# Turning the last block of outputs in two halves and storing it from two queues

## The chip, the cores and the metric

The kernel runs on one core of one Trainium2 chip. The metric is the device time of one execution in microseconds (us). The kernel before takes 943.23 us as the median of three runs (943.13 to 943.5). In this kernel TensorE does the matrix products, VectorE and ScalarE work on elements, and SyncE issues transfers. The program's tiles lie in two memories, SBUF and PSUM, and TensorE writes its products to tiles in PSUM. A transfer between SBUF and `out` is called a DMA, and the profile shows it as packets on 16 DMA engines (139,777 packets in the kernel before).

## The reference

An attention over pooled keys and values, followed by a feed-forward block with a snake activation. Cut to what matters:

```python
q, k, v: (8, 8, 576, 64)            # batch, heads, sequence, head dimension
k_p, v_p = mean of 8 neighbouring rows of k, v
x = softmax(q @ k_p.T / 8) @ v_p    # -> (4608, 512)
h = x @ w_in                        # w_in: (512, 2048)
g = h + sin(alpha * h)**2 / (alpha + 1e-9)
return g @ w_out                    # w_out: (2048, 512) -> out (4608, 512) float32
```

Only the end of the last product, `g @ w_out`, is touched by the change.

## The kernel before

The last product is computed for 8 groups of 576 output rows (`u`). Each group is made of 2 x 2 blocks by a scheme of seven products (`p`) with seven sub-products each, whose sums and differences are combined on VectorE. A finished block `t` lies in SBUF as 128 partitions (output columns, permuted) by `h` (2), `i` (2), `c` (T = 144 rows). VectorE turns it in 32 x 32 blocks into `o`, and four stores, one for each 32 partitions, write it to `out`:

```python
def out(u, i, j, t):
    o = self.op.tile([P, 2 * T // 32, 2, 32], F32, name="o", bufs=3)
    nc.vector.transpose(out=o[:].rearrange("p n h c -> p h n c"),
                        in_=t[:].rearrange("p h i c -> p h (i c)").rearrange("p h (n c) -> p h n c", c=32))
    r = u * self.S + i * 2 * T
    for a in range(4):
        c = j * 2 * P + a * 64
        nc.sync.dma_start(out=self.out[r:r + 2 * T, c:c + 64].rearrange("(n k) c -> k n c", k=32),
                          in_=o[32 * a:32 * a + 32].rearrange("k n h c -> k n (h c)"))
```

One store moves 72 KB in 288 pieces of 256 bytes (the trace has 1152 packets of 256 bytes for the last four). The block that ends last is that of the seventh product (`p == 3`), `i = 0, j = 1`:

```python
def early(st):                       # while the last products still run
    t = C[st["u"]]["c"]
    with_z(t, st["yz"])
    add(t[:, :, 1], t[:, :, 1], st["x1"][:])
# ... in combine(), for p == 3:
    t = c["c"]
    add(t[:, :, 0], t[:, :, 0], x[0][:])    # needs the last product; writes i = 0 of both h
    out(u, 0, 1, t)
# ... the order of the last products:
    fifth(); fourth()                # fourth() calls early(last)
    product(last, 2, last["x0"][:, 0, :], False)
    product(last, 3, last["x0"][:, 1, :], False)
    combine(last)
```

## Time and profile before

| | before |
|---|---|
| median time | 943.23 us |
| span, first to last instruction | 941.79 us |
| end of the last matmul | 936.07 us |
| from there to the end of the span ("the tail") | 5.72 us |
| TensorE busy | 98% of the span |

The tail is the number to follow, because the change touches nothing ahead of it. Its parts are read from the timeline, from the waits of the SyncE queue, and from the busy share of the DMA engines in stretches of 0.2 us. The lines of these views stand in the prediction.

### The profile page before, as it was taken

How to read it: one execution, taken by the hardware profiler on the slowest of the kernel's cores; microseconds unless marked ns; L12 is line 12 of the kernel's file. 1: busy time of each engine (PE TensorE's matmuls, PEld its weight loads, DVE VectorE, ACT ScalarE, POOL GpSimd, SP SyncE). 2: the span in 40 equal slices, each digit the busy share in tenths (PEclk: the TensorE clock that was granted, in tenths of full speed). 3: DMA queues.
4: the chain of work that ended last, by engine and by line, in shares of the span. 5: the costliest groups of instructions: out<-in, count | busy, mean ns of one | idle time of the engine just before them, and what ended most of it. 6: DMA issues, size and time to landing. Idle time of an engine off the chain costs nothing.

```text
span 941.8 us, 17546 instructions
## 1 busy us (share of the span) xinstructions
PE 920.8 (98%) x6859; PEld 819.5 (87%) x6859; DVE 694.5 (74%) x1043; ACT 445.6 (47%) x1042; POOL 197.9 (21%) x214
## 2 busy tenths in 40 slices
PE   5999999999999999999999999999999999999997
PEld 3687787887878878787888899999999999999997
DVE  5779584766748677484346889988989798889794
ACT  5477576585857758677696651212111111211111
POOL 1628354453634536250000000000000000000000
PEclk9999999999999999999999999999999999999999
DMA  9645457666576663745624545353435444343501
GB/s 230 178 142 173 122 190 167 201 160 201 154 195 194 167 191 101 186 148 146 224 90 143 187 141 150 103 164 89 148 105 135 118 127 127 117 135 93 160 13 38
DMA packets 139777, 137.82 MB, mean 146 GB/s; under 512 B 49024, under 2 KB 108176, under 8 KB 139696
## 3 DMA queue, kind: packets, MB, share of 16 engines
q1 hardware_dynamic: 138624, 135.53, 49.8%
q10 hardware_dynamic: 1072, 1.19, 0.5%
q8 instruction: 54, 0.88, 0.4%
q14 instruction: 27, 0.22, 0.1%
HBM read 74.46 MB, written 47.19 MB: 129 GB/s over the span
## 4 chain that ended last, share of the span: by engine, by line
PE 94%; DVE 2%; ACT 2%; DMA 1%; issue 0%; SPq 0%; ACTq 0%; DVEq 0%
PE bank L497 45%; PE bank L778 29%; PE ps_y L778 12%; PE ps_o L311 3%; PE ps_sc L210 2%; DMA q<-in_q_dram 1%; DVE as L373 1%; PE ps_qt L191 1%; PE ps_at L269 1%; ACT s L503 1%; PE bank L460 1%; DVE home L470 0%; PE ps_or L320 0%; PE bank L122 0%; DVE a L373 0%
## 5 line engine op out<-in xcount | busy, mean ns | idle before, releaser
L497 PE MATMUL bank<-home,a 128*128 128x256 f32 x1152 | 267.1, 383 | 0.8 <-ACT bank L535 0.8
L497 PEld LDWEIGHTS bank<-home,a 128*128 128x128 f32 x1152 | 214.8, 190 | 35.8 <-ACT bank L535 2.7
L497 PE MATMUL bank<-home,as 128*128 128x256 f32 x864 | 202.4, 383 | 1.2 <-DVE as L373 0.8
L497 PEld LDWEIGHTS bank<-home,as 128*128 128x128 f32 x864 | 161.2, 190 | 26.4 <-ACT bank L523 3.2
L107 POOL TENSOR_TENSOR kvin<-kvin 72x512 f32<-72x512 f32 x112 | 122.2, 1091 | 164.2 <-DMA kvin<-in_v_dram 108.8
L778 PE MATMUL bank<-s,wb 128*128 128x144 f32 x896 | 119.4, 286 | 0.4 <-ACT bank L891 0.4
L778 PEld LDWEIGHTS bank<-s,wb 128*128 128x128 f32 x896 | 113.7, 190 | 0.7 <-ACT bank L891 0.6
L510 ACT ACTIVATE s<-s,c 128x256 f32<-128x256 f32 (+1 forms) x216 | 110.0, 573 | 0.0
L503 ACT ACTIVATE s<-h,al 128x256 f32<-128x256 f32 x144 | 65.2, 501 | 79.6 <-DVE h L476 79.6
L476 DVE TENSOR_TENSOR h<-bank,p 128x512 f32<-128x512 f32 x72 | 49.2, 683 | 62.8 <-ACT s L510 28.2
L891 ACT COPY bank<-bank 128x144 f32<-128x144 f32 x56 | 14.7, 263 | 145.7 <-PE bank L778 144.3
L503 ACT ACTIVATE s<-bank,al 128x256 f32<-128x256 f32 x144 | 59.9, 467 | 33.5 <-PE bank L497 10.5
L564 DVE TENSOR_TENSOR h<-bank,s 128x512 f32<-128x512 f32 x36 | 24.6, 684 | 49.7 <-ACT s L510 49.0
L910 ACT COPY bank<-bank 128x144 f32<-128x144 f32 x56 | 14.7, 263 | 88.2 <-PE bank L778 88.2
L252 POOL TENSOR_TENSOR ex<-ex,sm 128x576 f32<-128x576 f32 (+1 forms) x38 | 42.7, 1148 | 60.0 <-DVE sm L251 29.1
L733 DVE TENSOR_TENSOR s<-r 128x576 f32<-128x576 f32 x64 | 48.1, 752 | 0.8
L564 DVE TENSOR_TENSOR h<-h,s 128x1024 f32<-128x1024 f32 x36 | 46.2, 1283 | 0.0
L733 DVE TENSOR_TENSOR s<-x 128x576 f32<-128x576 f32 x48 | 36.2, 753 | 7.6 <-PE ps_y L778 6.7
L868 ACT COPY bank<-ps_y 128x288 f32<-128x288 f32 x56 | 21.4, 383 | 38.7 <-PE ps_y L778 38.7
L147 DVE STREAM_TRANSPOSE tr<-q 128x1024 f32<-128x1024 f32 (+1 forms) x24 | 18.1, 808 | 26.8 <-DMA g_bridge<-h 21.3
L778 PE MATMUL bank<-s,a 128*128 128x144 f32 x256 | 36.6, 286 | 0.0
L778 PE MATMUL ps_y<-s,a 128*128 128x144 f32 x256 | 36.6, 286 | 0.0
(142 smaller groups left out, 1436.4 us busy)
## 6 DMA issues: line engine op xcount, KB each, us to landing
g_bridge<-h SPq DMA_DIRECT2D x72, 512.0 KB
r<-g_bridge SPq DMA_DIRECT2D x31, 1152.0 KB
out_dram<-o SPq DMA_DIRECT2D x128, 72.0 KB
q<-in_q_dram SPq DMA_DIRECT2D x8, 1024.0 KB
kvin<-in_k_dram SPq DMA_DIRECT2D x28, 288.0 KB
kvin<-in_v_dram SPq DMA_DIRECT2D x28, 288.0 KB
a<-in_moe_w_in_dram SPq DMA_DIRECT2D x16, 256.0 KB
q<-tr SPq DMA_DIRECT2D x48, 80.0 KB
```

Of the source, the lines that this page charges most:

```text
L107: (eng or nc.gpsimd).tensor_tensor(out=o, in0=t[:, :, 0:w], in1=t[:, :, w:2 * w], op=OP.add)
L210: nc.tensor.matmul(ps[e][r:r + q.shape[-1], hp, :], q[s], kb[s, hp, :], start=True, stop=True)
L252: eng.tensor_tensor(out=E(n, i, 0, H), in0=E(n, i, 0, H), in1=sm[:n].unsqueeze(2).to_broadcast([n, H, Sp]), op=OP.mult)
L311: nc.tensor.matmul(ps[64 * e:64 * e + 64, :], vp[:, h, :], x, start=True, stop=True)
L476: add = lambda o, x, y: nc.vector.tensor_tensor(out=o, in0=x, in1=y, op=OP.add)
L497: nc.tensor.matmul(ps[:, jj, :], self.A[p][:, kk, f * P:(f + 1) * P], x[:, kk, :], start=(start and jj == 0 and kk == 0), stop=(kk == 1), ...
L503: nc.scalar.activation(out=G.s[:, i, jj, j, :], in_=src[:, jj], func=AF.Sin, scale=self.al[:, f:f + 1])
L510: nc.scalar.activation(out=x, in_=x, func=AF.Square, scale=self.c[:, f:f + 1])
L564: add = lambda o, x, y: self.nc.vector.tensor_tensor(out=o, in0=x, in1=y, op=OP.add)
L733: tt = lambda o, x, y, op: nc.vector.tensor_tensor(out=o, in0=x, in1=y, op=op)
L778: nc.tensor.matmul(out, W[:, J // 2, J % 2, :], A[:, J, :], start=(start and J == 0), stop=(J == self.NJ - 1), skip_group_check=True)
L868: nc.scalar.copy(out=x0[:], in_=yz[:, 0:1, :].to_broadcast([P, 2, T]))
```

## The change

Its intent is to shorten the end: the last block is turned in two halves along `h`, and two of its four stores go to the queue of ScalarE, which is idle by then (its last copy ends at 932.45 us in the profile before).

```diff
             o = self.op.tile([P, 2 * T // 32, 2, 32], F32, name="o", bufs=3)
-            nc.vector.transpose(out=o[:].rearrange("p n h c -> p h n c"),
-                                in_=t[:].rearrange("p h i c -> p h (i c)").rearrange("p h (n c) -> p h n c", c=32))
+            end = (u, i, j) == (self.B - 1, 0, 1)
+            for h in (slice(0, 1), slice(1, 2)) if end else (slice(0, 2),):
+                nc.vector.transpose(out=o[:, :, h].rearrange("p n h c -> p h n c"),
+                                    in_=t[:, h].rearrange("p h i c -> p h (i c)").rearrange("p h (n c) -> p h n c", c=32))
             r = u * self.S + i * 2 * T
             for a in range(4):
                 c = j * 2 * P + a * 64
-                nc.sync.dma_start(out=self.out[r:r + 2 * T, c:c + 64].rearrange("(n k) c -> k n c", k=32),
+                (nc.scalar if end and a % 2 else nc.sync).dma_start(out=self.out[r:r + 2 * T, c:c + 64].rearrange("(n k) c -> k n c", k=32),
                                   in_=o[32 * a:32 * a + 32].rearrange("k n h c -> k n (h c)"))
```

## The prediction

Its rival (a) is that the issues of the two queues wait for each other; the pair of issues at 0.74 us is its test of that.

> **What bounds the kernel now.** I read the page first: the engine table, then the 40 slices, and after that only the end of the execution, because the diff touches nothing else (its condition is true for one block, the last of 32).
>
> ```profile
> PE 920.8 (98%) x6859; PEld 819.5 (87%) x6859; DVE 694.5 (74%) x1043; ACT 445.6 (47%) x1042; POOL 197.9 (21%) x214
> ```
>
> TensorE is busy for 98% of a span of 941.8 us. So the body is bound by matmuls, and a change that leaves them alone can only win in the few microseconds at the end in which TensorE has nothing left. The timeline of the last microseconds shows that stretch (start, duration, engine, line, operation):
>
> ```profile
> 934.93 1.14 PE L778 MATMUL bank<-s,wb 128*128 128x144 f32 x8
> 936.11 0.45 DVE L733 TENSOR_TENSOR cc<-cc,bank 128x288 f32<-128x288 f32 x1 [0.32 <-PE bank L778]
> 936.60 0.78 DVE L796 STREAM_TRANSPOSE o<-cc 128x576 f32<-128x576 f32 x1
> 937.40 1.85 SPq L801 DMA_DIRECT2D out_dram<-o  x4
> ```
>
> The last matmul ends at 936.07, then one add, one transpose and four stores follow strictly one after another, with gaps of 0.02 to 0.04 us. The stores' issue ends at 937.40 + 1.85 = 939.25. Cut finer, the four issues are one of 0.32 us (start 937.40) and three of about 0.46 to 0.47 (starts 937.76, 938.26, 938.78). What follows is in the waits of the SyncE queue after 930 us, and in the stretches of 0.2 us (columns: length, busy time of PE, weight load, DVE, ACT, POOL, clock, busy share of the 16 DMA engines, GB/s):
>
> ```profile
> SPq L1012 <- DMA out_dram<-o: 1.4, 1, 1.4
> ```
>
> ```profile
> 938.00:938.20 0.20, 0.00 (x0) 0.00 (x0) 0.00 (x0) 0.00 (x0) 0.00 (x0) 1.00 0.00 0
> 938.20:938.40 0.20, 0.00 (x0) 0.00 (x0) 0.00 (x0) 0.00 (x0) 0.00 (x0) 1.00 0.58 133
> 938.40:938.60 0.20, 0.00 (x0) 0.00 (x0) 0.00 (x0) 0.00 (x0) 0.00 (x0) 1.00 0.87 181
> 938.60:938.80 0.20, 0.00 (x0) 0.00 (x0) 0.00 (x0) 0.00 (x0) 0.00 (x0) 1.00 0.40 85
> ...
> 939.60:939.80 0.20, 0.00 (x0) 0.00 (x0) 0.00 (x0) 0.00 (x0) 0.00 (x0) 0.50 0.45 90
> 939.80:940.00 0.20, 0.00 (x0) 0.00 (x0) 0.00 (x0) 0.00 (x0) 0.00 (x0) 0.50 0.78 177
> 940.00:940.20 0.20, 0.00 (x0) 0.00 (x0) 0.00 (x0) 0.00 (x0) 0.00 (x0) 0.50 0.78 160
> 940.20:940.40 0.20, 0.00 (x0) 0.00 (x0) 0.00 (x0) 0.00 (x0) 0.00 (x0) 0.50 0.10 18
> ```
>
> The data starts about 938.23, so 0.83 after the first issue begins, and stops about 940.22. The share of the engines goes up and down with the issues: they are not kept full. Summed over all eleven stretches (0.58, 0.87, 0.40, 0.87, 0.70, 0.50, 0.89, 0.45, 0.78, 0.78, 0.10 = 6.92, times 0.2 us) the four stores cost 1.38 us of engine time, 0.346 each, but are handed over only every 0.49 us. So the tail is paced by the issue on one queue, and about 30% of the engines' time in it is idle. SyncE is released at about 940.66 and the span ends at 941.8; those last 1.1 us are the closing barrier, which the change doesn't touch. The chain view names an earlier store ahead of the last transpose; I don't believe it, since the timeline shows the add ending just there.
>
> [...] The trace agrees that issue time is real here (1.85 us of a 3.3 us stretch from first issue to release). [...] The trace before has one place to test it, the very start:
>
> ```profile
> 0.74 0.40 ACTq L333 DMA_DIRECT2D s<-in_moe_alpha_dram  x1
> 0.74 0.42 SPq L102 DMA_DIRECT2D home<-in_k_dram  x1
> ```
>
> Both begin together and neither is longer than it is alone (ScalarE's other issue, a load at 554.1, is 0.40 too)[...]; but the ScalarE load is of 8 KB in 16 rows, a weak test. [...] adds of 128x576 take about 0.755 us and of 128x288 about 0.455.
>
> **The change part by part.** *Transposes.* The compiled order has two transposes of 128x9x32 in place of one of 128x2x9x32. They are cut along h, but the last add writes both h, and each store reads both h of its 32 partitions. So neither half can start before the add ends, and no store can start before the second half ends: nothing is overlapped, and the cut only costs. Halving an add saves 0.755 - 0.455 = 0.30 us, so I take 0.778 - 0.30 = 0.478 for half a transpose (estimate). Two independent DVE instructions in a row overlap by about 0.08 in their windows (two 0.45 us adds show as 0.82). Pair: 2 x 0.478 - 0.08 = 0.876, against 0.778: **+0.10 us**, all on the path.
>
> *Stores.* Two of four issues move to ScalarE, idle since 932.45 (its last copy starts 932.19 and takes 0.26), so nothing stands ahead of them. Their waits in the compiled order are the transpose and two DMA semaphores last used by stores of at least ten microseconds before or by the block at 927, long landed. Let t be the first issue's start. Before: last issue ends t+1.85, data ends t+2.82. After: SyncE ends its two at t+0.32+0.04+0.46 = t+0.82, ScalarE at most t+0.9 (0.40 for its first). The second pair's data could then start at about t+0.82+0.5 = t+1.3. But two stores' data need 2 x 0.346 = 0.69 us from t+0.83, so until t+1.52 at the least: the pair is in time and the engines become the pace. All four: t+0.83+1.38 = t+2.21 with full engines, t+0.83+1.38/0.88 = t+2.40 at the 0.87 to 0.89 that the fullest stretches show. Middle t+2.30: **-0.52 us**. It isn't the 0.95 us by which the issues shorten, for the data now limits.
>
> *Sum:* +0.10 - 0.52 = **-0.42 us**, hence 943.23 - 0.42 = 942.8.
>
> **The rivals.** (a) [...] The two queues wait for each other and the four stores still come every 0.49 us. For it: [...]the first issue of 0.32 against 0.46 for those right behind it, as if something were being waited for. Against: the pair at 0.74. Time: +0.10, so 943.3. I give it 25%. (b) *Interleaving hurts.* The stores write neighbouring 256-byte pieces of the same output rows, and two queues would mix them; the engines' 1.38 us might grow. For it: nothing in the trace tests two queues of stores; against: the same 16 engines carried up to 406 GB/s near 559 us with larger pieces. Time: around 943.1. 15%. (c) *Engines drain better with both queues full,* under 0.346 per store: up to -0.7, so 942.5. 10%. (d) *The transposes hide,* or the compiler gains from the halves: excluded by the order of the add and the reads of the stores.
>
> **Range and chances.** Half the weight at 942.8, a quarter at 943.3, the rest around gives a mean near 942.9. Three runs before spread over 0.37 us (943.13 to 943.5), as much as the effect. Range 942.3 to 943.5. 2% is 18.9 us, and the whole tail after the last matmul is 941.8 - 936.07 = 5.7 us, so faster by over 2% is not possible by this path; slower would need a disturbance elsewhere, and all matmuls stand in the same order. Within 2%: 0.99.
>
> **What would show it.** In the profile after: two transposes of about 0.48 us with the first at the end of the add, the stores starting about 0.1 later relative to the last matmul (right), or one of them earlier (wrong). Two issues on SyncE and two on ScalarE starting together near 937.5, each 0.3 to 0.47 long; issues of 0.7 or more on either would show rival (a). Stretches of 0.2 us with a share near 0.9 without dips, ending 2.2 to 2.4 us after the first issue, would show the engines as the new pace; a summed share time well above 1.38 us would show (b). I'd be wrong if the data ends later than t+2.6, or if the span before 936 us moves.

## The result

The changed kernel takes 943.28 us (942.28 to 943.65, 4 runs), the kernel before in the same rounds 943.37 us (943.13 to 944.28, 4 runs). The ratio is 0.9996 with a 95% interval of 0.9978 to 1.0013. It is the mean time of one kernel's fast runs over that of the other's in the same rounds, so not quite the ratio of the two medians. By total time the two are the same.

The end of the profile is not the same. The timeline of the changed kernel, in which the two queues' issues are given by further looks at shorter windows (start, duration, engine, line, operation):

```profile
934.92 1.14 PE L778 MATMUL bank<-s,wb 128*128 128x144 f32 x8
936.10 0.46 DVE L733 TENSOR_TENSOR cc<-cc,bank 128x288 f32<-128x288 f32 x1 [0.32 <-PE bank L778]
936.59 0.84 DVE L798 STREAM_TRANSPOSE o<-cc 128x288 f32<-128x288 f32 x2
937.46 0.89 ACTq L803 DMA_DIRECT2D out_dram<-o  x2
```

```profile
937.46 0.32 SPq L803 DMA_DIRECT2D out_dram<-o  x1
937.46 0.38 ACTq L803 DMA_DIRECT2D out_dram<-o  x1
...
937.82 0.46 SPq L803 DMA_DIRECT2D out_dram<-o  x1
937.88 0.47 ACTq L803 DMA_DIRECT2D out_dram<-o  x1
```

The last matmul ends at 936.07, as before. The two halves take 0.84 us in place of 0.78, back to back. The issues on the two queues lie side by side, and all four are done at 938.35, where one queue had been busy until 939.25. The stretches of the DMA engines (columns as in the prediction; the last two are the busy share and GB/s) show what became of it:

```profile
938.20:938.40 0.20, 0.00 (x0) 0.00 (x0) 0.00 (x0) 0.00 (x0) 0.00 (x0) 1.00 0.33 74
938.40:938.60 0.20, 0.00 (x0) 0.00 (x0) 0.00 (x0) 0.00 (x0) 0.00 (x0) 1.00 0.91 196
938.60:938.80 0.20, 0.00 (x0) 0.00 (x0) 0.00 (x0) 0.00 (x0) 0.00 (x0) 1.00 0.91 192
938.80:939.00 0.20, 0.00 (x0) 0.00 (x0) 0.00 (x0) 0.00 (x0) 0.00 (x0) 1.00 0.81 132
939.00:939.20 0.20, 0.00 (x0) 0.00 (x0) 0.00 (x0) 0.00 (x0) 0.00 (x0) 1.00 0.81 132
939.20:939.40 0.20, 0.00 (x0) 0.00 (x0) 0.00 (x0) 0.00 (x0) 0.00 (x0) 1.00 1.17 254
939.40:939.60 0.20, 0.00 (x0) 0.00 (x0) 0.00 (x0) 0.00 (x0) 0.00 (x0) 1.00 1.17 257
939.60:939.80 0.20, 0.00 (x0) 0.00 (x0) 0.00 (x0) 0.00 (x0) 0.00 (x0) 1.00 0.97 208
939.80:940.00 0.20, 0.00 (x0) 0.00 (x0) 0.00 (x0) 0.00 (x0) 0.00 (x0) 1.00 0.15 31
```

The dips to 0.40 to 0.50 between stores are gone: from 938.4 to 939.8 the share never falls under 0.8, and the data ends in the stretch that begins at 939.8 instead of the one at 940.2. By the records, the tail is 5.17 us (941.23 - 936.07) against 5.72: **0.55 us shorter**, somewhat more than the 0.42 us that the sum of the prediction gave. The next question is whether this is real, which of the two parts makes it, and why the total time doesn't show it.

### The profile page after: what moved, and what is told of

It is laid out like the page before. It is cut to its first block, busy times and chain, and to the rows that moved or that the text cites. A ratio compares the mean times of both kernels' runs of the same rounds, so it can differ in the third digit from the quotient of the medians.

```text
span 941.2 us, 17548 instructions
## 1 busy us (share of the span) xinstructions
PE 921.0 (98%) x6859; PEld 819.7 (87%) x6859; DVE 692.9 (74%) x1044; ACT 445.9 (47%) x1042; POOL 199.1 (21%) x214
## 3 DMA queue, kind: packets, MB, share of 16 engines
q10 hardware_dynamic: 1680, 1.34, 0.6%
## 4 chain that ended last, share of the span: by engine, by line
PE 95%; DVE 2%; ACT 1%; DMA 1%; issue 0%; SPq 0%; DVEq 0%; ACTq 0%
PE bank L497 45%; PE bank L778 29%; PE ps_y L778 12%; PE ps_o L311 3%; PE ps_sc L210 2%; DMA q<-in_q_dram 1%; PE ps_qt L191 1%; PE ps_at L269 1%; PE bank L460 1%; DVE as L373 0%; DVE home L470 0%; PE ps_or L320 0%; PE bank L122 0%; ACT s L503 0%; PE bank L210 0%
## 5 line engine op out<-in xcount | busy, mean ns | idle before, releaser
L778 PE MATMUL ps_y<-r,wb 128*128 128x144 f32 x256 | 36.6, 286 | 0.0
L778 PE MATMUL bank<-r,wb 128*128 128x144 f32 x256 | 36.6, 286 | 0.0
```

Of the source, the lines that this page charges most:

```text
L778: nc.tensor.matmul(out, W[:, J // 2, J % 2, :], A[:, J, :], start=(start and J == 0), stop=(J == self.NJ - 1), skip_group_check=True)
```

## The experiments

The theory: the halves cost a few hundredths and bring nothing; the second queue brings the whole gain, because one queue hands over a store only about every 0.5 us while the engines need 0.35 us for it; with two queues the data itself is the pace. The rivals: the halves let something start sooner; the issues of the two queues wait for each other; neighbouring pieces written by two queues disturb each other.

Four kernels ran on one chip, four more on the same chip, and the two that are cut by rows on another. This table gathers the profiles of all but the last three, which have their own sections; times from the records in us, "issue" is the start of the first of the last block's stores after the end of the last matmul, "data" the time from the first to the last packet of these stores, "engine time" the sum of their packets' durations divided by 16 (up to 24 packets are under way at once on the 16 engines in the changed kernel, so it is not quite the time in which the engines were busy).

| kernel | last matmul ends | span | tail | issue | data | engine time |
|---|---|---|---|---|---|---|
| before | 936.07 | 941.79 | 5.72 | 1.33 | 2.08 | 1.39 |
| before, again | 936.14 | 941.86 | 5.72 | 1.33 | 2.08 | 1.39 |
| halves alone | 936.64 | 942.39 | 5.74 | 1.39 | 2.05 | 1.38 |
| two queues alone | 936.24 | 941.38 | 5.14 | 1.33 | 1.68 | 1.43 |
| changed kernel | 936.07 | 941.23 | 5.17 | 1.39 | 1.64 | 1.44 |
| changed kernel, again | 937.58 | 942.75 | 5.17 | 1.39 | 1.65 | 1.44 |
| short stores, one queue | 935.41 | 940.91 | 5.51 | 1.39 | 1.82 | 0.78 |
| short stores, two queues | 935.64 | 940.21 | 4.57 | 1.39 | 1.11 | 0.78 |
| pairs apart | 936.13 | 941.36 | 5.23 | 1.39 | 1.72 | 1.53 |

### Do the tails repeat? Both kernels unaltered

> The kernel before unaltered, for a second profile: shows how well the tail repeats. Expected tail 5.7 us within 0.1. If it differs by 0.3 or more, the tail of a single profile can't carry the comparison.

> The changed kernel unaltered, in more rounds. If the gain of 0.6 us of the one profile is real: tail again 5.1 to 5.2 us, and a ratio of times near 0.9994. If the profile was chance: tail nearer 5.7, ratio 1.000.

Measured: the tails repeat to a hundredth (5.72 and 5.72; 5.17 and 5.17). The gain in the tail is real. The total times are another matter: the changed kernel took 942.5 us as a median of 5 runs (941.35 to 944.54), before 943.55 us (942.94 to 944.55, 9 runs), ratio 0.9990 with an interval of 0.9977 to 1.0002, which still holds 1. The table shows why: the last matmul, whose time no edit of the tail can move, ends anywhere between 935.41 and 937.58. The second profile of the changed kernel has the *longer* span of all, and its last matmuls show where this comes from:

```profile
936.44 1.14 PE L778 MATMUL bank<-s,wb 128*128 128x144 f32 x8
938.11 0.84 DVE L798 STREAM_TRANSPOSE o<-cc 128x288 f32<-128x288 f32 x2
```

It ends its matmuls at 937.58, 1.51 us later than its twin. Setting the matmuls of these two profiles side by side by number, the second is 0.9 us late at 61 us and 1.5 us late from 118 us on, where the lag stays within 0.06 us. Most of it comes very early: 1.1 us of lag is there after 11 us, and the waits of TensorE in the first 110 us show 6.6 us in place of 5.3 for VectorE's `kp` (L179). Over the profiles of all twelve kernels, the matmul numbered 101 starts anywhere between 20.0 and 22.1 us, and one near the end, numbered 6801, between 928.0 and 930.2. So most of the scatter between executions arises at the start of the kernel, and it is several times the effect in the tail.

### Halves alone

```diff
-                (nc.scalar if end and a % 2 else nc.sync).dma_start(out=...
+                nc.sync.dma_start(out=...
```

> The last transpose in two halves, all four stores on SyncE as before. The tail is the time from the end of the last matmul to the end of the span: 5.73 us before, 5.14 after. My theory (the halves only cost, the second queue brings the gain): the pair of halves lasts 0.84 us as in the changed kernel instead of 0.78, stores come every 0.49 us as before, tail 5.73 + 0.06 = 5.8 us. Rival (the halves let something start sooner): the first store starts under 1.3 us after the last matmul, tail under 5.5 us. Total time: same as before within noise for both.

The timeline of this kernel:

```profile
937.17 0.84 DVE L798 STREAM_TRANSPOSE o<-cc 128x288 f32<-128x288 f32 x2
938.03 1.85 SPq L803 DMA_DIRECT2D out_dram<-o  x4
```

The pair takes 0.84 us, the issue of the four stores 1.85 us as before, and it starts 1.39 us after the last matmul in place of 1.33. The tail is 5.74 us, 0.02 more than before: of the 0.06 us the data phase, shorter by 0.03, gave some back; what shortened it is not shown. Time 944.17 us (943.0 to 944.34, 5 runs), ratio 1.0003 (0.9991 to 1.0016). The halves bring nothing.

### Two queues alone

```diff
-            for h in (slice(0, 1), slice(1, 2)) if end else (slice(0, 2),):
+            for h in (slice(0, 2),):
```

> One whole transpose as before, two of the four last stores on ScalarE. My theory: issues on both queues start together, tail 5.14 - 0.06 = 5.1 us, so a little better than the full change. Rival (the gain needs the halves): tail near 5.7 us. Total time: 0.6 us under before, 0.0006 of it, perhaps not visible.

```profile
936.76 0.78 DVE L798 STREAM_TRANSPOSE o<-cc 128x576 f32<-128x576 f32 x1
937.57 0.82 SPq L803 DMA_DIRECT2D out_dram<-o  x2
937.57 0.89 ACTq L803 DMA_DIRECT2D out_dram<-o  x2
```

One transpose of 0.78 us, the two queues side by side, and a tail of 5.14 us, the best of the first six rows. Time 943.16 us (942.55 to 943.72, 5 runs), ratio 0.9995 (0.9982 to 1.0009). The whole gain is the second queue's; the rival that needs the halves has fallen.

### What sets the pace: stores of 5/9 the size

Both kernels give a wrong result on purpose: only 5 of the 9 row blocks of the last block are stored. The one-queue kernel has, besides, `nc.sync` for all four stores.

```diff
-                ....dma_start(out=self.out[r:r + 2 * T, c:c + 64]....,
-                              in_=o[32 * a:32 * a + 32]....)
+                ....dma_start(out=self.out[r:r + 32 * m, c:c + 64]....,      # m = 5 for the last block, else 9
+                              in_=o[32 * a:32 * a + 32, 0:m]....)
```

> Wrong result on purpose: the last block's four stores each write only 5 of their 9 row blocks (40 KB in place of 72), all on SyncE; transposes in halves as in the changed kernel. Before, the DMA engines work on these stores for 2.08 us from first to last packet. My theory (one queue is paced by its issues, every 0.49 us): still about 1.9 us, only the last store's own data gets shorter (0.346 x 4/9 = 0.15 us). Rival (the data sets the pace with one queue already): 2.08 x 5/9 = 1.2 us.

> Wrong result on purpose: the same short stores, two on SyncE and two on ScalarE. In the changed kernel the engines work on the last stores for 1.65 us. My theory (with two queues the data sets the pace): about 1.65 x 5/9 = 0.9 us. Rival (with two queues issue[...] still sets it): 1.4 us or more. The two short runs together: with one queue the length hardly follows the data, with two it does.

First one queue, then two, a part of each in stretches of 0.2 us (the last two columns are the engines' share and GB/s):

```profile
938.20:938.40 0.20, 0.00 (x0) 0.00 (x0) 0.00 (x0) 0.00 (x0) 0.00 (x0) 1.00 0.64 132
938.40:938.60 0.20, 0.00 (x0) 0.00 (x0) 0.00 (x0) 0.00 (x0) 0.00 (x0) 1.00 0.11 23
938.60:938.80 0.20, 0.00 (x0) 0.00 (x0) 0.00 (x0) 0.00 (x0) 0.00 (x0) 1.00 0.74 159
938.80:939.00 0.20, 0.00 (x0) 0.00 (x0) 0.00 (x0) 0.00 (x0) 0.00 (x0) 1.00 0.17 32
```

```profile
938.00:938.20 0.20, 0.00 (x0) 0.00 (x0) 0.00 (x0) 0.00 (x0) 0.00 (x0) 1.00 0.92 194
938.20:938.40 0.20, 0.00 (x0) 0.00 (x0) 0.00 (x0) 0.00 (x0) 0.00 (x0) 1.00 0.67 136
938.40:938.60 0.20, 0.00 (x0) 0.00 (x0) 0.00 (x0) 0.00 (x0) 0.00 (x0) 1.00 0.88 190
```

With one queue, 44% less data shortens the data phase by 13% (2.08 to 1.82 us), and the engines stand nearly idle (0.11, 0.17) between stores: the issue is the pace. Of the 0.27 us, 0.15 is the last store's own data (0.53 us from its first to its last packet, now 0.38), and 0.09 comes from issues that are themselves a little shorter (0.44 us in place of 0.46 to 0.47). With two, the phase shortens by 33% (1.65 to 1.11 us): much more, but not the 44% that I expected if only the data counted. The small dip to 0.67 shows where the rest is. A pair of short stores needs about 2 x 0.78 / 4 = 0.39 us of engine time, no more than the 0.36 to 0.42 us between two issues of a queue, so here issue and data are level. A pair of full stores needs 2 x 1.44 / 4 = 0.72 us, well over it. That the data is the pace with full stores therefore holds; for short ones it no longer does.

The packets show this directly, if they are counted off to the stores in the order of each queue. With one queue, each full store sends its first packet 0.51 to 0.53 us after its issue has ended. In the changed kernel SyncE's second store sends its first packet only 0.84 us after its issue, which is 0.02 us after the last packet of SyncE's first store: it waits for the data ahead of it. In the short kernel with two queues it is 0.50 us again, and 0.10 us pass between the two stores' data.

### Do neighbouring pieces disturb each other?

```diff
-                (nc.scalar if end and a % 2 else nc.sync).dma_start(...
+                (nc.scalar if end and a // 2 else nc.sync).dma_start(...
```

> As the changed kernel, but SyncE stores the 64-column groups 0 and 1 and ScalarE 2 and 3, so that the two stores under way at once do not write neighbouring 256-byte pieces of a row. In the changed kernel the packets of the last stores took 1.44 us summed over 16 engines, 1.39 before. Rival (neighbouring pieces on two queues disturb each other): the sum falls back to 1.39 and the data phase from 1.65 to under 1.6 us. My theory (a little more waiting per packet whenever two queues are busy, wherever they write): 1.44 and 1.65 again.

Measured: neither. The engine time rises to 1.53 us, the data phase to 1.72 and the tail to 5.23 us. With pieces that are not neighbours under way at once, the packets took *longer*, so neighbours on two queues are no disturbance. My own theory, that the place doesn't matter, is missed too, by 0.09 us of engine time. This is one profile, and the edit also changes which SBUF partitions the two stores under way read, so why it is so stays open.

### Making the halves useful: the add cut as well

If the halves are to help, the last add must be cut along `h` too, for its first half is ready one product earlier.

```diff
     product(last, 2, last["x0"][:, 0, :], False)
+    # last block only: add h = 0 and turn it here
     product(last, 3, last["x0"][:, 1, :], False)
     combine(last)      # last block: add h = 1, turn it, store (two queues)
```

> As the changed kernel, but the last add is cut along the same halves, and the first half (whose product is ready 1.1 us before the last matmul ends) is added and turned before it ends. In the changed kernel the stores' issue starts 1.40 us after the last matmul. Rival (the halves are right, only the add kept them from helping): 1.1 us or less. My estimate: the free time of VectorE before the last matmul ends is only 0.3 us, and two adds of 144 columns (0.31 each) with two half transposes (0.46 each) make 1.6 us from 935.8 on, so the issue again starts about 1.4 us after the last matmul: no gain.

The timeline:

```profile
935.20 0.67 DVE L733 TENSOR_TENSOR cc<-cc,bank 128x288 f32<-128x288 f32 x2
935.90 0.48 DVE L799 STREAM_TRANSPOSE o<-cc 128x288 f32<-128x288 f32 x1
...
935.92 1.25 PE L778 MATMUL bank<-s,wb 128*128 128x144 f32 x8 [0.97 <-DVE cc L733]
937.21 0.30 DVE L733 TENSOR_TENSOR cc<-cc,bank 128x144 f32<-128x144 f32 x1 [0.83 <-PE bank L778]
937.54 0.48 DVE L799 STREAM_TRANSPOSE o<-cc 128x288 f32<-128x288 f32 x1
938.05 0.89 ACTq L806 DMA_DIRECT2D out_dram<-o  x2
```

Neither expectation saw this. The single add of 144 columns took 0.30 us, close to the estimated 0.31, and the stores' issue does start only 0.88 us after the last matmul, but the last eight matmuls now start 0.97 us late: they write the other half of the PSUM tile that VectorE is reading, and wait for that add (it ends at 935.87, they start at 935.92). Measured from ScalarE's last copy, which starts at 932.18 in the changed kernel and at 932.05 here, the span ends 9.05 us later there and 9.85 us here: the cut add costs 0.8 us in this pair of profiles. A PSUM tile for each half was not tried.

### A cut that helps: by rows

The rows of `i = 1` are complete before the last add. So row blocks 5 to 8 can be turned and stored while the last product runs, and only 5 of 9 blocks are left for after it.

```diff
+    # in early(), last group: turn and store row blocks 5 to 8, two stores a queue
     add(t[:, :, 0], t[:, :, 0], x[0][:])
-    out(u, 0, 1, t)
+    out(u, 0, 1, t, 0, 5, True)     # row blocks 0 to 4, two stores a queue
```

> The last block is cut by rows and not by h: row blocks 5 to 8 need only values that are ready before the last add, so they are turned and stored (two stores a queue) while the last product runs; after the last add only blocks 0 to 4 are turned and stored (two stores a queue, 40 KB each). In the compiled order the SyncE stores of the second part wait for the semaphores of ScalarE's early stores (eight semaphores go round). If that wait matters: those stores start only when the early ones have landed, some 2.0 us after their issue at 936.3, so about 2.4 us after the last matmul in place of 1.40, and the tail is 5.5 us or more, no better than the 5.17 of the change. If it doesn't matter: issue 1.15 us after the last matmul, tail about 4.4 us.

The timeline of the end, and the waits of the SyncE queue after 931 us:

```profile
936.82 1.84 ACTq L804 DMA_DIRECT2D out_dram<-o  x4
...
938.56 0.32 SPq L804 DMA_DIRECT2D out_dram<-o  x1
939.00 0.37 SPq L804 DMA_DIRECT2D out_dram<-o  x1
```

```profile
SPq L804 <- DMA out_dram<-o: 0.9, 1, 0.9
```

ScalarE issues its part 1.19 us after the last matmul. SyncE can't: its store waits 0.9 us for a DMA, because the compiled program gives its semaphore (the counter that tells of a DMA's landing) to one of the early stores of ScalarE first, and starts 1.96 us after the last matmul. The wait is real but shorter than I had put it (the early store had landed 1.74 us after its issue, not 2.0 or more), and the tail is 4.88 us, between the two outcomes. Time 942.8 us (4 runs), ratio 0.9987 (0.9973 to 1.0).

Storing the block before this one from both queues as well (behind ScalarE's last copy, so that TensorE doesn't wait for it: its profile shows no wait of TensorE after 925 us) changes the round of the eight semaphores (the traces of the kernel before and of the changed one show landings on eight, numbers 100 to 105, 109 and 110):

```diff
-                    out(u, 1, 1, c["a"])
+                    out(u, 1, 1, c["a"], q="SASA" if u == self.B - 1 else "SSSS")   # S: SyncE, A: ScalarE
```

> As the cut by rows, but the block before the last is stored from both queues too, which changes the round of the semaphores: in the compiled order the last stores now wait for semaphores of stores issued 3 us before. Expected: last transpose (320 columns, about 0.5 us) ends 1.13 us after the last matmul, 0.27 less than in the changed kernel; data of 5/9 the size takes about 0.9 us from first to last packet in place of 1.65. Tail about 5.17 - 0.27 - 0.5 (SyncE's part of the data phase) = 4.4 us, 1.3 us under the kernel before, ratio of times near 0.9986. If the early stores hold up the last ones on the DMA engines, the tail is 4.8 or more. The matmuls must end where they did, as ScalarE's stores stand behind its last copy.

```profile
936.00 1.76 SPq L806 DMA_DIRECT2D out_dram<-o  x4
936.00 1.84 ACTq L806 DMA_DIRECT2D out_dram<-o  x4
936.34 0.51 DVE L801 STREAM_TRANSPOSE o<-cc 128x320 f32<-128x320 f32 x1
```

Both queues now issue their four stores without a stop. The last matmul ends at 935.77, the last transpose 1.08 us after it, the last stores' issue starts 1.11 us after it, and the tail is 4.38 us: 1.34 us under before and 0.79 under the changed kernel, as expected (4.4). The sum agrees better than its parts: the data of the last stores took 1.06 us from first to last packet and not 0.9, and the check that ends last waits for ScalarE's last store (0.37 us after its last packet), not for SyncE's. Time 941.93 us (941.08 to 943.16, 5 runs) against 944.01 us (943.26 to 945.45, 9 runs), ratio 0.9978 (0.9965 to 0.9992). It is the only kernel whose interval lies wholly below 1, though far from a difference of 2%. Of the 0.22%, about 2.1 us, the tail explains 1.34; the rest is within the interval and can be scatter of the body.

## Why the prediction was right or wrong

The time, 942.9 us, and its range of 942.3 to 943.5 hold the measured median of 943.28. That alone says little, and is in part luck: the prediction took the scatter of three runs, 0.37 us, but nine later runs of the kernel before lie between 942.94 and 944.55, and five of the changed kernel between 941.35 and 944.54, which is wider than the range. The steps, checked in the tail, say more.

- *The bound.* Right. TensorE's last matmul ends where it did, and the change in the tail is the change in the span (0.56 us in the first pair of profiles).
- *Transposes, +0.10.* Right in kind, a little too high: 0.84 us for the pair, +0.06. I took the half from adds at 0.478; the first half took 0.479, but the second only 0.434 to 0.435. The halves alone gained nothing, as argued from the add and the stores' reads.
- *Stores, -0.52.* Right in kind, somewhat too small. From the first issue to SyncE's release the records give 3.27 us before and 2.65 after, **-0.61**. Three of its terms were off and partly cancelled, so that the size came near is partly luck. The end of the data before was read as 2.82 after the first issue, from the share of the last stretch; the last packet ends at 2.91. The data phase after was predicted to end at 2.30; it ends at 2.47, since the packets took longer (1.44 us of engine time for 1.39) and the share falls to 0.81 in two stretches. So the data gives -0.44, less than predicted. But release doesn't follow the end of all data. The data of SyncE's own stores ends at 2.29, and SyncE is released 0.36 later, as it was before (0.36 after its last packet); ScalarE's ends 0.175 later still, and the checks that follow SyncE's release come at the same spacing as before (0.05 to 0.07 us apart in both), so none of them had to wait. That is the other 0.175. That ScalarE's part hides behind these checks is inferred from this spacing.
- *Sum, -0.42.* Measured in the tail: -0.55 in both pairs of profiles.
- *Rival (a), the queues wait for each other.* Wrong. The two queues' first issues start 4 ns apart and take 0.32 and 0.38 us, no longer than alone. Nor is such a wait seen behind the issues: ScalarE's first packet comes 0.67 us after its issue has ended, and for its lone load at 554 us it was 0.66. (The prediction's own test, at 0.74 us, was weaker than it says: SyncE's issue took 0.42 us there, and its next three of that line 0.33 to 0.39.)
- *Rival (b), interleaving hurts.* The engine time did grow, by 0.05 us (1.39 to 1.44), but writing apart made it grow more (1.53), not less. So neighbouring pieces are not its cause.
- *Rival (c), engines drain better with both queues full.* Partly: stretches of 254 and 257 GB/s with shares of 1.17 stand against at most 192 GB/s before, but the stretches at 132 GB/s took it back. The 0.87 to 0.89 that the prediction took for the fullest share was no ceiling; a share of 1.03 also stands in the kernel before, from 557 to 558 us, during one queue's load.
- *Chances.* Within 2% was the outcome, for the reason given.

## What to carry to other kernels

When a kernel ends in several small stores, ask whether the DMA engines' share dips between them. Here it fell from 0.87 to 0.89 down to 0.40 to 0.50, the issuing queue was the pace (issues every 0.49 us for 0.35 us of engine time a store; the short stores confirmed it), and a second, idle queue gained until the data was the pace. This was 0.55 us of 943, too little for the total to show. When you split an operation, ask whether the parts become ready at different times and whether their readers need only one part; here the cut along rows had that property (1.34 us off the tail, with the block before stored from both queues) and the cut along `h` had not (0.02 us onto it). And measure such an edit in the tail of the trace, where it repeated to 0.01 us here, not in a total that scatters by one or two.
